# Fewer dummy matmuls, state weights over all rows, merged row sums and a new written-out order in a fused cross-attention and mixer kernel

## The chip, the core and the metric

The kernel runs on one core of a Trainium2 chip. The metric is the device time of one execution in microseconds, as the median of several runs; smaller is better. A profile of one execution gives a span (from the first to the last recorded instruction), and that execution has a time of its own, a little longer than its span.

The engines are named as in the profile: PE is TensorE's matrix multiply and PEld its loading of the stationary operand, DVE is VectorE, ACT is ScalarE, POOL is GpSimd, and SP is SyncE, which here only issues transfers.

## The reference

For each of 8 batches there are 8 heads with 512 tokens of x (64 wide) and 32 state rows (64 wide). Both directions of attention are computed, each as a plain softmax:

```python
scores = scale * np.matmul(x, state.transpose(0, 1, 3, 2))      # [8, 8, 512, 32]
a = softmax(scores); xread = np.matmul(a, state)
scores2 = scale * np.matmul(state, x.transpose(0, 1, 3, 2))     # the same products, transposed
a2 = softmax(scores2); sread = np.matmul(a2, x)
y = concat([xread, sread])  ->  [8, 544, 512]                    # heads side by side
wq = y @ w_q; wk = y @ w_k                                       # 512 -> 64
mixed = (scale * wq @ wk.T) @ y
out = np.maximum(mixed, 0.0) @ w_out                             # [8, 544, 512], float32
```

## The kernel before

Everything is done per batch b, in bfloat16 operands with float32 sums. The steps are small functions, and the kernel's whole order is a text, ORDER: a list of tokens `name.b.engine`. They are issued one by one, and each engine works through its own instructions strictly in that order, waiting where an operand or a buffer is not there yet. The last letter of a token says where or how: p is POOL, v DVE, a ACT, s a store by SP; for TensorE's steps t multiplies with a stationary operand of 128 columns, c with two of 64 columns side by side (the helpers `mm`, lines 161 and 163, and `tr`, lines 170 and 174), and r means that the step has one form only. There is no scheduler behind it: which work stands ahead of which on each engine is what the text says.

The steps of a batch are these. `ix` loads x through POOL's queue and casts it (for batch 0, four smaller loads and the casts `xc`). `xT0` and `xT1` transpose four heads each, eight 128x128 transposes, and `xTe` evicts them from PSUM. `pt0`, `pt1` are the scores, `exp0`, `exp1` their exponentials on ACT, without a maximum, into E. `rs` adds E over the 32 state rows on DVE (a token with a digit takes half of it, one without a digit all), `rinv` inverts the sums, and `A` on POOL multiplies: the attention of the tokens. `at` transposes A, `ate` evicts it. `sums` and `srd` make the attention of the state rows: column sums of E and E transposed times x. `srn` normalises them on DVE, `sbd` spreads them over blocks on POOL, `srT` transposes them.

The mixer doesn't form y for the tokens. It multiplies A with small matrices instead: `sw` (line 246) are the state rows times w_q and w_k, `wq`, `wk` and `wks` the projections, `g` is A transposed times wk, `v` combines it with the block-spread state (`stbd`, made once per batch on POOL) into a 64x512 matrix V, and `mix0`, `mix1`, `mixs` are V with wq, of which `mxe` and `mse` take the positive part. `fin0` to `fin3` multiply that with w_out, 128 tokens of 512 columns each, in four matmuls of 512 columns; two of them share a PSUM tile that `oe` evicts together and `os` stores with 512 KB. `fix` is the same for one piece, evicted and stored alone by `oc` with 256 KB; the very last piece (`oc3.7.b`) is halved between DVE and ACT. `fs` does the state rows of four batches at a time.

`stt` transposes the states of one to three batches; `ste` and `stf` evict its two halves into `stT`. In `stT` a head of the first half of the heads occupies rows 0 to 63, one of the second half rows 64 to 127, and the other 64 rows are zero (`zst`).

`fill` (line 155) issues dummy matmuls of zeros, 512 columns each, as many as the token's number. Their results aren't used.

PSUM is divided into two pools: psA with two tiles of two banks (dummies, `sw`, `mix` and `fin`), and psB with four of one bank (all else). A step that needs a tile waits until the former tenant of its place has been evicted. The single pieces pass through a pool in SBUF, tail, with seven buffers.

Of the kernel before, what the change touches and what calls it, by code (L numbers as in the profile page):

```python
# [13 lines left out]


ORDER = """
zst.0.p ix1.0.p stc.0.v xc1.0.a fill.1.t stt.0.c ste.0.v stbd.0.p stf.0.a xc0.0.p xc3.0.v ix2.0.p
fill.7.t xT0.0.t xc2.0.v xTe0.0.a fill.1.t xT1.0.t is.0.p stc.1.v fill.1.t stt.1.c xTe1.0.v stbd.2.p
fill.1.t pt0.0.t stf.1.v fill.1.t pt1.0.t exp0.0.a ste.1.v iwo.0.p exp1.0.a rs0.0.v fill.4.t
sums.0.t ix3.0.p rinv0.0.v wc.0.a fill.1.t xT0.1.t rs1.0.v fill.1.t srd.0.r xTe0.1.v A0.0.p fill.1.t  # L20
xT1.1.t fill.1.t sw.0.r xTe1.1.a rinv1.0.v fill.1.t pt0.1.t srn.0.v A1.0.p at0.0.t srT.0.t exp0.1.a
pt1.1.t srTe.0.v sbd.0.p swe.0.a xT0.2.t rs0.1.v at1.0.t exp1.1.a xT1.2.t xTe0.2.v stbd.1.p ate.0.a
xTe1.2.v fill.1.t stt.2.c stt.3.c rs1.1.v ste.2.a pt0.2.t stbd.6.p stf.3.v exp0.2.a fill.1.t wq.0.c
ste.3.v wks.0.c ix4.0.p stf.2.a wk.0.t rs0.2.v sw.3.r pt1.2.t wke.0.v swe.3.a stbd.3.p sw.1.r
rinv.1.v exp1.2.a g.0.t sw.2.r ge.0.v stbd.5.p swe.1.a rs1.2.v sums.2.t v.0.c wqe.0.a rinv.2.v
xT1.3.c swe.2.a A.1.p ve.0.v xT0.3.c xTe1.3.a srd.2.r xTe0.3.v mix0.0.r mix1.0.r mxe0.0.v sums.1.t
mxe1.0.a A.2.p srd.1.r at.1.t pt1.3.t srn.1.v ate.1.a fin0.0.t srn.2.v ix5.0.p xT1.4.t exp1.3.a
srT.1.t xT0.4.t xTe1.4.v srTe.1.a fin1.0.t sbd.1.p xTe0.4.a rs1.3.v pt1.4.t wq.1.c sbd.2.p exp1.4.a
wks.1.c wqe.1.v pt0.4.t oe0.0.a srT.2.t wk.1.t rs1.4.v at.2.t ix6.0.p fin2.0.t ate.2.v wke.1.a
os0.0.s exp0.4.a stbd.7.p g.1.t srTe.2.v fin3.0.t ge.1.v rs0.4.v sums.4.t stbd.4.p oe1.0.a srd.4.r  # L30
rinv.4.v v.1.c srn.4.v wq.2.c A.4.p ve.1.a os1.0.s srT.4.c wks.2.c wk.2.t srTe.4.a mixs.1.r wke.2.v
mix1.1.r wqe.2.a mix0.1.r mse.1.v xT1.5.t mxe0.1.a ix7.0.p at.4.t xTe1.5.v g.2.t xT0.5.t mxe1.1.a
ge.2.v sbd.4.p pt1.5.t xTe0.5.v v.2.c exp1.5.a fin2.1.c ve.2.v pt0.5.c rs1.5.v mixs.2.r mix1.2.r
exp0.5.a ate.4.v xT1.6.c mse.2.a sums.5.c fin3.1.c xTe1.6.a rs0.5.v rinv.5.v xT0.6.c mxe1.2.a
oe1.1.v A.5.p pt1.6.c wq.4.c srd.5.r exp1.6.a mix0.2.r srn.5.v os1.1.s fin0.1.c mxe0.2.a rs1.6.v
sbd.5.p xT0.7.c xTe0.6.v fin0.2.c xTe0.7.a wqe.4.v pt0.6.c srT.5.c at.5.c exp0.6.a xT1.7.c ate.5.v
srTe.5.a fin1.2.c xTe1.7.a rs0.6.v wq.5.c rinv.6.v wks.5.c wk.5.c wqe.5.a pt1.7.c A.6.p wke.5.v
wks.4.c sums.6.c exp1.7.a srd.6.r g.5.t oe0.2.a rs1.7.v wk.4.t pt0.3.t fin1.1.t srn.6.v exp0.3.a
os0.2.s wke.4.v sbd.6.p at.6.t oe0.1.a rs0.3.v srT.6.t g.4.t fin2.2.t ate.6.v os0.1.s fin3.2.t
ge.5.v ge.4.v srTe.6.v v.5.c oe1.2.a rinv.3.v wq.6.c ve.5.v A.3.p wks.6.c wk.6.c v.4.c os1.2.s  # L40
wke.6.a wqe.6.v mix1.5.r ve.4.a mixs.5.r mix0.5.r mxe1.5.v sums.3.t mxe0.5.a g.6.t srd.3.r mixs.4.r
ge.6.v mix0.4.r mse.5.a mix1.4.r srn.3.v mxe0.4.a v.6.c mse.4.v sbd.3.p srT.3.c pt0.7.c srTe.3.v
at.3.c mxe1.4.a ve.6.v fin2.5.c ate.3.v exp0.7.a fin3.5.c rs0.7.v wq.3.c oe1.5.a wks.3.c fin0.4.c
rinv.7.v A.7.p wqe.3.a os1.5.s mix0.6.r mixs.6.r wk.3.t mse.6.a fin1.4.t wke.3.a mxe0.6.a g.3.t
oe0.4.v at.7.t sums.7.t ate.7.a srd.7.r mix1.6.r srn.7.v os0.4.s fin2.4.c mxe1.6.v sbd.7.p srT.7.c
fin3.4.c srTe.7.a ge.3.v fin2.6.c oe1.4.v v.3.c fin3.6.c ve.3.v os1.4.s fin0.5.c oe1.6.a fin1.5.c
os1.6.s mix1.3.r oe0.5.v mixs.3.r wq.7.c mxe1.3.a wks.7.c wk.7.c mixs.0.r mse.3.v mix0.3.r os0.5.s
mse.0.a wke.7.v fin0.6.c wqe.7.a mxe0.3.a g.7.c fin1.6.c ge.7.a fin0.3.c oe0.6.v fin1.3.c os0.6.s
v.7.c oe0.3.a fin2.3.c ve.7.a fin3.3.c os0.3.s mix0.7.r oe1.3.a mixs.7.r fs.3.t mxe0.7.v mse.7.a
os1.3.s mix1.7.r fse.3.v fs.7.t mxe1.7.a fse.7.v fix1.7.t fix2.7.t oc1.7.a fix0.7.t oc2.7.a fix3.7.t  # L50
oc0.7.a oc3.7.b
"""


# [1 line left out]
def kernel(  # L56
# [20 lines left out]
    NP = H // 2  # L77
# [3 lines left out]

    const = ctx.enter_context(tc.tile_pool(name="const", bufs=1))
    work = ctx.enter_context(tc.tile_pool(name="work", bufs=4))
    tail = ctx.enter_context(tc.tile_pool(name="tail", bufs=7))
    psA = ctx.enter_context(tc.tile_pool(name="psA", bufs=2, space=bass.MemoryType.PSUM))
    psB = ctx.enter_context(tc.tile_pool(name="psB", bufs=4, space=bass.MemoryType.PSUM))

# [4 lines left out]
    stT = const.tile([128, B, 2, H, NS], BF, name="stT")  # L92
    stbd = const.tile([128, B, 2, NP, D], BF, name="stbd")
    w_f = const.tile([128, NP, 2, DH], FP, name="w_f")
    w_qk = const.tile([128, NP, 2, DH], BF, name="w_qk")
    w_o = const.tile([128, KC, DM], BF, name="w_o")
    sw = const.tile([128, B, 2, 2, DH], BF, name="sw")
# [143 lines left out]
    def sw_mm(n, p, e):  # L241
        ps = psA.tile([128, 2, 512], FP, name="sw_ps", tag="psA")
        for bb in range(2):
            for q in range(NP):
                for r in range(2):
                    nc.tensor.matmul(
                        out=ps[NS * q : NS * q + NS, r, 2 * DH * bb : 2 * DH * bb + 2 * DH],
                        lhsT=stT[64 * r : 64 * r + 64, 2 * p + bb, r, NP * r + q, :],
                        rhs=w_qk[64 * r : 64 * r + 64, q, 0:2, :],
                        start=True,  # L250
                        stop=True,
                    )
        G["sw", p] = ps
# [363 lines left out]
    def fs_ev(n, b, e):  # L617
# [7 lines left out]
        "zst": zeros, "stt": st_tr, "ste": st_ev, "stf": st_ev,  # L625
        "stbd": stbd_blk, "fill": fill, "fix": fin_mm, "os": fin_st,
        "sw": sw_mm, "swe": sw_ev, "xT": xT_mm, "xTe": xT_ev, "xs": x_dT, "as": a_dT, "pt": pt_mm, "exp": pt_exp,
        "rs": rs, "rinv": rv, "A": nrm, "at": at_mm, "ate": at_ev,
        "srd": srd, "sums": sums, "srn": srn, "sbd": sbd, "srT": srT_mm, "srTe": srT_ev,
# [38 lines left out]
```

## Time and profile before

| | us |
|---|---|
| median of 5 runs | 88.06 (87.75 to 88.66) |
| the profiled execution | 87.74 |
| its span | 86.0 |
| PE busy in the span | 80.2 (1579 matmuls) |
| DVE, ACT, POOL busy | 52.6, 56.0, 45.1 |
| dummy matmuls of `fill` | 23 |
| output written, from the first store's issue at 28.5 on | 8.91 MB |

The page shows busy times, a picture of the span in 40 slices, the chain of work that ended last, and groups of equal instructions with their mean length. A matmul's row shows the time from its start to its modelled end, and neighbours overlap; the distance from one group's start to the next is what the group costs in a stream. A shape such as 128*64 behind the tiles' names is that of the stationary operand: rows times columns.

### The profile page before, as it was taken

What the parts mean: (1) busy time and instruction counts of PE and PEld (TensorE: products, weight loads), DVE (VectorE), ACT (ScalarE), POOL (GpSimd) and SP (SyncE); (2) the same over time, 40 slices, a digit from 0 to 9 for tenths busy, and PEclk for the clock granted to TensorE, in tenths of its full rate; (3) what the DMA queues carried; (4) which work ended last, traced back from release to release, by engine and by line L of the source; (5) the groups of instructions that cost most, each with busy time, mean ns of one, the idle gap of its engine ahead of it and who ended that gap; (6) DMA issues with size and microseconds to landing.
All of it is one profiled execution on the core that took longest, in us unless ns stands there. A gap on an engine that the chain in (4) does not pass through costs nothing.

```text
span 86.0 us, 3560 instructions
## 1 busy us (share of the span) xinstructions
PE 80.2 (93%) x1579; PEld 53.1 (62%) x1579; DVE 52.6 (61%) x111; ACT 56.0 (65%) x83; POOL 45.1 (52%) x58
## 2 busy tenths in 40 slices
PE   4999999999999999999999999999999999999900
PEld 1336567778877688778689657865755565534400
DVE  2238864998956857887766958880687355055010
ACT  1634539989789678588887838968921591765530
POOL 7999979999999969308508653408050000000000
PEclk9999999999999999999999999999999999999999
DMA  0899999999519999992600565102362662567782
GB/s 10 284 324 188 199 193 192 198 189 162 82 12 150 132 138 345 273 165 31 252 0 11 213 278 208 44 8 111 133 236 95 274 280 105 238 250 293 294 312 78
DMA packets 15119, 15.00 MB, mean 175 GB/s; under 512 B 3712, under 2 KB 12672, under 8 KB 15104
## 3 DMA queue, kind: packets, MB, share of 16 engines
q0 software_dynamic: 9104, 4.36, 40.6%
q1 hardware_dynamic: 4880, 8.98, 28.2%
q10 hardware_dynamic: 1120, 1.44, 4.6%
q8 instruction: 12, 0.20, 0.9%
q14 instruction: 3, 0.02, 0.1%
HBM read 10.22 MB, written 8.91 MB: 223 GB/s over the span
## 4 chain that ended last, share of the span: by engine, by line
PE 79%; DMA 9%; ACT 4%; POOL 3%; issue 1%; DVE 1%; POOLq 0%
PE fin_ps L161 21%; PE fin_ps L163 12%; DMA x_bf<-in_x_dram 9%; PE mix_ps L541 5%; PE xT_ps L174 5%; PE xT_ps L170 3%; PE srd_ps L369 3%; PE at_ps L174 3%; PE v_ps L505 3%; PE fins_ps L163 2%; PE g_ps L163 2%; PE wq_ps L433 2%; PE v_ps L514 2%; POOL stT L201 2%; PE pt_ps L163 2%; PE wk_ps L163 2%
## 5 line engine op out<-in xcount | busy, mean ns | idle before, releaser
L346 POOL TENSOR_TENSOR A<-E,rinv 128x1024 bf16<-128x1024 bf16 (+1 forms) x9 | 15.4, 1720 | 11.8 <-DVE rinv L340 11.3
L161 PE MATMUL fin_ps<-w_o,rmix 128*64 128x512 bf16 x160 | 19.4, 380 | 0.0
L142 ACT COPY ost<-fin_ps 128x1024 f32<-128x1024 f32 (+2 forms) x13 | 11.2, 864 | 11.6 <-PE fin_ps L161 5.9
L148 ACT ACTIVATE rmix<-mix_ps 128x1024 bf16<-128x1024 f32 x12 | 12.1, 1024 | 2.5 <-PE mix_ps L541 2.4
L144 DVE COPY ost<-fin_ps 128x1024 f32<-128x1024 f32 (+1 forms) x6 | 6.5, 1091 | 9.9 <-PE fin_ps L163 5.4
L407 POOL TENSOR_TENSOR sbd<-srn,mask 128x256 bf16<-128x256 bf16 x16 | 9.4, 613 | 6.0 <-DVE srn L397 5.9
L161 PEld LDWEIGHTS <-rmix 128*64 128x64 bf16 x160 | 8.4, 110 | 6.2 <-issue 0.6
L163 PE MATMUL fin_ps<-w_o,rmix 128*128 128x512 bf16 x48 | 11.7, 379 | 0.0
L332 DVE TENSOR_REDUCE rsum<-E 128x16 f32<-128x512 bf16 x16 | 10.8, 675 | 0.9 <-ACT E L317 0.7
L317 ACT ACTIVATE E<-pt_ps 128x512 bf16<-128x512 f32 x16 | 9.5, 601 | 2.4 <-PE pt_ps L161 1.3
L234 POOL TENSOR_TENSOR stbd<-st_bf,mask 128x256 bf16<-128x256 bf16 x16 | 9.3, 610 | 0.4 <-DVE st_bf L144 0.2
L142 ACT COPY xT<-xT_ps 128x1024 bf16<-128x1024 bf16 x7 | 7.1, 1012 | 3.0 <-PE xT_ps L174 2.3
L144 DVE COPY xT<-xT_ps 128x1024 bf16<-128x1024 bf16 x9 | 6.2, 688 | 2.0 <-PE xT_ps L174 1.8
L155 PE MATMUL fill_ps<-zero 128*128 128x512 bf16 x23 | 7.3, 381 | 0.0
L150 DVE TENSOR_SCALAR rmix<-mix_ps 128x1024 bf16<-128x1024 f32 x4 | 4.9, 1222 | 3.4 <-PE mix_ps L541 3.4
L163 PEld LDWEIGHTS <-rmix 128*128 128x128 bf16 x48 | 4.3, 98 | 4.0 <-ACT rmix L148 0.2
L183 POOL DMA_DIRECT2D x_bf<-in_x_dram x7 | 6.6, 949 | 0.0
L174 PE MATMUL xT_ps<-ident,x_bf 128*128 128x128 bf16 x80 | 6.0, 219 | 0.3 <-ACT E L317 0.2
L174 PEld LDWEIGHTS <-x_bf 128*128 128x128 bf16 x80 | 4.9, 98 | 1.7 <-issue 0.5
L541 PE MATMUL mix_ps<-wq,V 64*128 64x256 bf16 x64 | 5.8, 272 | 0.0
L132 PE MATMUL warm_ps<-zero 128*128 128x512 bf16 x8 | 3.4, 597 | 1.2 <-DVE mask L133 1.2
L163 PE MATMUL pt_ps<-stT,xT 128*128 128x64 bf16 x88 | 4.4, 193 | 0.0
(90 smaller groups left out, 139.8 us busy)
## 6 DMA issues: line engine op xcount, KB each, us to landing
out_dram<-ost SPq DMA_DIRECT2D x14, 512.0 KB, 2.7
x_bf<-in_x_dram POOLq DMA_DIRECT2D x7, 512.0 KB, 7.7
out_dram<-ost ACTq DMA_DIRECT2D x3, 256.0 KB, 2.1
x_f<-in_x_dram ACTq DMA_DIRECT2D x2, 256.0 KB, 3.9
x_f<-in_x_dram SPq DMA_DIRECT2D x2, 256.0 KB, 4.3
w_o<-in_moe_w_out_dram POOLq DMA_DIRECT2D x1, 512.0 KB, 8.5
out_dram<-ost SPq DMA_DIRECT2D x2, 256.0 KB, 2.4
st_bf<-in_state_dram POOLq DMA_DIRECT2D x1, 160.0 KB, 7.9
```

The costliest lines, as they stand in the source:

```text
L142: nc.scalar.copy(out=out, in_=in_)
L144: nc.vector.tensor_copy(out=out, in_=in_)
L148: nc.scalar.activation(out=out, in_=in_, func=AF.Relu)
L161: nc.tensor.matmul(out=out[64 * h : 64 * h + 64], lhsT=lh, rhs=rhs, **kw)
L163: nc.tensor.matmul(out=out, lhsT=lhsT, rhs=rhs, **kw)
L174: nc.tensor.transpose(out=out, in_=in_, identity=ident)
L234: nc.gpsimd.tensor_tensor(out=stbd[:, b, r], in0=st_bf[:, b, r : r + 1, :].to_broadcast((128, NP, D)), in1=mask[:, :, None].to_broadcast(( ...
L317: nc.scalar.activation(out=L[b]["E"][:, r].rearrange("p c q n -> p c (q n)"), in_=L[b][f"pt{r}"], func=AF.Exp, scale=float(scale),)
L332: nc.vector.reduce_sum(out=L[b]["rsum"][:, w], in_=L[b]["E"].rearrange("p r c q n -> p (r c q) n")[:, w], axis=AX.X,)
L346: eng.tensor_tensor(out=L[b]["A"].rearrange("p r c q n -> p (r c q) n")[:, w], in0=L[b]["E"].rearrange("p r c q n -> p (r c q) n")[:, w], ...
L407: nc.gpsimd.tensor_tensor(out=L[b]["sbd"][:, r], in0=L[b]["srn"][:, r : r + 1, :].to_broadcast((128, NP, D)), in1=mask[:, :, None].to_broa ...
L541: nc.tensor.matmul(out=ps[:, h, kk, :], lhsT=L[b]["V"][rows, 128 * k : 128 * k + 128], rhs=L[b]["wq"][rows, 0:SH], start=True, stop=True,)
```

## The change

There are three edits.

1. The order text is a new one. It has 14 dummy matmuls instead of 23, none of them behind the first transposes of batch 1. For batches 3 to 7 the two half row sums `rs0`, `rs1` are one step `rs`. Of the output pieces, two each of batches 5 and 6 are now single ones (`fix`, `oc`) beside the four of batch 7, eight in all. Most steps change places, some the engine (a `v` for an `a` or the reverse), and some TensorE steps the form (t or c).
2. In `sw_mm` the stationary operand and the moving one span all 128 rows instead of the 64 that aren't zero.
3. The pool tail has 12 buffers instead of 7.

Nothing else differs; line numbers after the order text are lower by two.

The core of the diff, with the parts of the order that are spoken of:

```diff
-zst.0.p ix1.0.p stc.0.v xc1.0.a fill.1.t stt.0.c ste.0.v stbd.0.p stf.0.a xc0.0.p xc3.0.v ix2.0.p
-fill.7.t xT0.0.t xc2.0.v xTe0.0.a fill.1.t xT1.0.t is.0.p stc.1.v fill.1.t stt.1.c xTe1.0.v stbd.2.p
-fill.1.t pt0.0.t stf.1.v fill.1.t pt1.0.t exp0.0.a ste.1.v iwo.0.p exp1.0.a rs0.0.v fill.4.t
-sums.0.t ix3.0.p rinv0.0.v wc.0.a fill.1.t xT0.1.t rs1.0.v fill.1.t srd.0.r xTe0.1.v A0.0.p fill.1.t
-xT1.1.t fill.1.t sw.0.r xTe1.1.a rinv1.0.v fill.1.t pt0.1.t srn.0.v A1.0.p at0.0.t srT.0.t exp0.1.a
-pt1.1.t srTe.0.v sbd.0.p swe.0.a xT0.2.t rs0.1.v at1.0.t exp1.1.a xT1.2.t xTe0.2.v stbd.1.p ate.0.a
...
-v.7.c oe0.3.a fin2.3.c ve.7.a fin3.3.c os0.3.s mix0.7.r oe1.3.a mixs.7.r fs.3.t mxe0.7.v mse.7.a
-os1.3.s mix1.7.r fse.3.v fs.7.t mxe1.7.a fse.7.v fix1.7.t fix2.7.t oc1.7.a fix0.7.t oc2.7.a fix3.7.t
-oc0.7.a oc3.7.b
+zst.0.p ix1.0.p stc.0.v fill.1.t stt.0.c stbd.0.p stf.0.a ste.0.a xc1.0.a xc0.0.p xc3.0.v ix2.0.p
+fill.5.t xT0.0.t xc2.0.v fill.1.t xT1.0.t xTe0.0.v is.0.p stc.1.v fill.1.t pt0.0.t xTe1.0.v stbd.2.p
+fill.1.t stt.1.c exp0.0.a stf.1.v fill.1.t pt1.0.t ste.1.a rs0.0.v iwo.0.p exp1.0.a rinv0.0.v A0.0.p
+rs1.0.v fill.4.t xT0.1.t wc.0.a xT1.1.t rinv1.0.v sums.0.t xTe0.1.v A1.0.p srd.0.r sw.0.r xTe1.1.v
+at0.0.t swe.0.a pt0.1.t ix3.0.p srn.0.v at1.0.t xT0.2.t exp0.1.a ate.0.v srT.0.t sbd.0.p xT1.2.t
+xTe0.2.a srTe.0.v pt1.1.t xTe1.2.v wq.0.c exp1.1.a stbd.6.p wks.0.c rs0.1.v wk.0.t wqe.0.a stt.2.c
+wke.0.v sums.1.t ste.2.a stbd.1.p pt1.2.t stf.2.v g.0.t srd.1.r exp1.2.a ge.0.v sw.1.r srn.1.v
+ix4.0.p v.0.c swe.1.a rs1.1.v stt.3.c ve.0.a sw.2.r rinv.1.v sbd.1.p srT.1.t pt0.2.t stf.3.a swe.2.v
+mix0.0.r mixs.0.r exp0.2.a mix1.0.r mse.0.v A.1.p xT1.3.t ste.3.v mxe1.0.a sums.2.t srTe.1.v xT0.3.t
+xTe1.3.v srd.2.r mxe0.0.a sw.3.r xTe0.3.v ix5.0.p pt1.3.t at.1.t srn.2.v swe.3.a fin2.0.t rs1.2.v
...
+exp1.7.a ate.5.v exp0.7.a g.4.t at.6.t ge.4.v srT.6.t fin3.2.t srTe.6.v ate.6.v v.4.c oe1.2.v wq.6.c
+ve.4.a sums.7.c wq.5.c wks.5.c wqe.6.v wqe.5.a mix1.4.r os1.2.s mix0.4.r rs.7.v mxe1.4.a mixs.4.r
+srd.7.r wks.6.c wk.5.c wk.6.c wke.5.a fin2.3.c mxe0.4.v mse.4.a wke.6.a g.5.c fin3.3.c srn.7.v
+ge.5.a rinv.7.v sbd.7.p srT.7.c v.5.c oe1.3.v srTe.7.a g.6.c ve.5.a fin0.3.c A.7.p ge.6.v fin1.3.c
...
+wke.7.v mix0.6.r wqe.7.a mix1.6.r mxe0.6.v fix3.5.c mxe1.6.a fix2.5.c mse.5.v fse.3.v g.7.c fin0.6.c
+ge.7.a oc2.5.v fin1.6.c oc3.5.v fin0.5.c oe0.6.a fin1.5.c os0.6.s v.7.c oe0.5.a fix2.6.c ve.7.v
+os0.5.s mixs.6.r mixs.7.r oc2.6.a mix1.7.r mse.6.v mix0.7.r mse.7.v mxe1.7.a fix3.6.t mxe0.7.v
+fs.7.t oc3.6.a fix2.7.t fse.7.a fix1.7.t oc2.7.a fix0.7.t oc1.7.a fix3.7.t oc0.7.a oc3.7.b
...
-    tail = ctx.enter_context(tc.tile_pool(name="tail", bufs=7))
+    tail = ctx.enter_context(tc.tile_pool(name="tail", bufs=12))
...
-                        lhsT=stT[64 * r : 64 * r + 64, 2 * p + bb, r, NP * r + q, :],
-                        rhs=w_qk[64 * r : 64 * r + 64, q, 0:2, :],
+                        lhsT=stT[:, 2 * p + bb, r, NP * r + q, :],
+                        rhs=w_qk[:, q, 0:2, :],
```

## The prediction

> **What bounds the kernel now.** I read the page's busy times first, then the chain that ended last, then TensorE's instructions in order of time.
>
> ```profile
> PE 80.2 (93%) x1579; PEld 53.1 (62%) x1579; DVE 52.6 (61%) x111; ACT 56.0 (65%) x83; POOL 45.1 (52%) x58
> PE   4999999999999999999999999999999999999900
> PEclk9999999999999999999999999999999999999999
> ```
>
> TensorE is busy in every slice but the first and the last two, at full clock; no other engine passes 65%. The chain in order of time says where it is held and where it runs free:
>
> ```profile
> 3.00 7.73 DMA x_bf<-in_x_dram
> ...
> 10.77 0.62 PE xT_ps L174 x8
> ...
> 78.42 3.47 PE fin_ps L163 x16
> 81.89 0.02 issue
> 81.92 0.44 DVE ost L144
> ...
> 82.38 0.37 ACT ost L142
> ```
>
> The reader should see three parts: 10.77 us until the second batch of x has landed (issued by POOL at 3.00), 71.1 us of TensorE, and 4.1 us from 81.89 to the span's end at 86.0 for the last eviction and its store. The windows confirm the middle (width, then busy time and count of TensorE, its weight loads, DVE, ACT and POOL):
>
> ```profile
> 10.77:20.50 9.73, 9.41 (x246) 7.13 (x248) 7.42 (x17) 8.02 (x14) 9.14 (x15) 1.00 1.48 188
> 30.00:40.00 10.00, 10.00 (x282) 8.14 (x282) 7.83 (x15) 7.92 (x12) 5.64 (x6) 1.00 1.09 205
> 70.00:81.90 11.90, 11.88 (x106) 5.66 (x102) 3.74 (x4) 6.92 (x11) 0.00 (x0) 1.00 0.62 245
> ```
>
> So the end moves with TensorE's own work, plus waits, after 10.77. TensorE's timeline prices that work, by the distance from one group's start to the next:
>
> ```profile
> 18.33 0.31 PE L246 MATMUL sw_ps<-w_qk,stT 64*32 64x128 bf16 x16
> 18.57 0.41 PE L163 MATMUL pt_ps<-stT,xT 128*128 128x64 bf16 x8
> 18.90 0.31 PE L246 MATMUL sw_ps<-w_qk,stT 64*32 64x128 bf16 x16
> ...
> 31.40 0.39 PE L433 MATMUL wq_ps<-AT,sw 128*64 128x256 bf16 x4
> 31.62 0.28 PE L442 MATMUL wq_ps<-srT,w_qk 128*64 128x32 bf16 x8
> ...
> 46.74 0.40 PE L163 MATMUL wk_ps<-sw,AT 128*128 128x64 bf16 x8
> 46.98 0.40 PE L163 MATMUL pt_ps<-stT,xT 128*128 128x64 bf16 x8
> 47.21 1.03 PE L163 MATMUL fin_ps<-w_o,rmix 128*128 128x512 bf16 x4
> 48.08 0.61 PE L174 MATMUL at_ps<-ident,A 128*128 128x128 bf16 x8
> ```
>
> pt takes 0.23 us (46.98 to 47.21) where its neighbours use the array whole (128*128), but 0.33 (18.57 to 18.90) before a group in the shape 64*32. Each change of this shape (written after the tiles' names) costs about 0.105 us. With that one number and a base per group (fin 0.865, xT and at 0.447, pt, wk and g 0.23 whole or 0.25 in halves, mix 0.225, v 0.44, wq 0.335, wks 0.13, srd 0.25, sw 0.135, dummy 0.216) I added up the order from 10.77: 64.30 of groups and 54 changes x 0.105 = 5.67 give 80.74. The trace ends at 81.89; the 1.15 between are 0.17 for the last matmul's run-out, some 0.6 of waits before 20.5 (0.34 for an exponential at 14.42, 0.3 at 17.7) and 0.36 of small ones later. The sum follows the trace within 0.1 from 20.5 to 70, so I trust it for the new order.
>
> **What the Trainium skill says.** "TensorEngine Tiling (Array Packing)", section Tiling Modes (Key Properties): changing the tiling mode, not just the tile, drains TensorE. The trace agrees, at 0.105 us, also between column modes. "TensorE: Matmul & The Clock Gate", section Part 2 (Back-to-back issue gap): N/2.4 + 2.5 ns warm, 56 ns for N=128; eight xT transposes in 0.45 us agree. Its Part 1 says that an idle window of about 3.4 us halves the clock; the clock row shows none. "Runtime: NRT & Kernel Launch", section Instruction fetch mechanics: instructions come in 16 KiB blocks of 256, ahead of use. The page's 12 instruction packets of 0.20 MB agree; their 0.9% of 16 engines' span is 1.03 us each, and TensorE spends over 3 us on a block. No wait of before needs fetch as its cause, so I give the "instruction fetch" side of the new order nothing, in either direction (at most 0.3 if one late block was inside the small waits).
>
> **The change part by part.**
>
> *Dummies.* 23 become 14. Three of the nine lie before 10.77, where the x load holds TensorE: nothing. The six later ones are 6 x 0.216 = 1.30 of stream. sums.0 (0.18) moves from before 10.77 to after it. Ahead of it ACT now evicts the first state before it casts its share of x (done about 6.4, not 4.8), but the first exponential still starts near 8.5 and A for batch 0 near 10.5; the cover is the x load's 10.77, with 0.3 to spare.
>
> *Order after 10.77.* Shape changes fall from 54 to 41: 13 x 0.105 = 1.37. Of these, three lie ahead of xT1.3 (the first transposes of batch 3) and ten behind it. Halved and whole groups trade for a few hundredths.
>
> *Column-tiled state weights (L246).* sw now contracts all 128 rows (the other half of stT is zero), in shape 128*32. Before, r=0 and r=1 ran in different row tiles: 16 matmuls in 0.135. Now r, the innermost loop, puts two successive matmuls on the same 32 columns, and matmuls start in order: per bb and q one 53 ns stream more, 8 x 53 = 0.43 us. The trace does not show this form; bounds are 0.21 (four abreast throughout, 16 x 53 / 4) and 0.85 (one by one). I take 0.43: +0.30 each, three times ahead of xT1.3, once behind. That it stands next to srd (also 128*32) saves shape changes, counted above.
>
> *Merged row sums.* Five pairs of L332 (675 ns each for 512 elements) become one of 1024. DVE's ost evictions take 0.686 for 512 and 1.224 for 1024 elements, so 0.54 for the second half: 1.21 instead of 1.35. DVE has room: nothing by itself, but a longer piece ahead of what is queued behind it, see below.
>
> *Moved loads.* ix3 is now behind both halves of A for batch 0 on POOL, issued about 12.7 instead of 9.89. It took 10.3 us to land (20.2), behind the w_o load (issued 9.08, landed 17.6) on one queue; from 12.7 it is still queued before w_o has landed, so again 20.2. The cover is w_o; without it, the 6.6 to 7.7 us of the other x loads still give 20.4 at worst. ix6 and ix7 come at 28.8 and 34 by POOL's list (A 1.91, sbd 1.19, stbd 1.18, load 0.94 each), landing about 36 and 41.4; TensorE wants them at 37.1 and 42.0. Little slack.
>
> *Late pieces singly, deeper tail buffers.* Two more pairs of pieces (batches 5 and 6) go through psB singly: two 512 KB stores become four of 256, two evicted by DVE and stored by SP, two by ACT (0.59, and 0.36 of issue on its queue). SP's list holds stores alone, in the order of their evictions, so none stands long behind a later one. At the end ACT is through with its last whole piece when DVE is through with its half of the split one, as before: the 4.1 us tail stays. I take nothing, bounded by -0.2 (less in flight) and +0.3 (the last 14 pieces now come in 13.4 us, 274 GB/s, near the 312 that the page reaches).
>
> *Sum to xT1.3.* New order from 10.77: 7.13 of groups, 12 changes (1.26), 0.89 for three slower sw: 20.05. Waits: 0.2 for batch 2 (5.86 + 7.7 = 13.56), and at the end the buffer of pt0.2, freed by its exponential, which on ACT stands behind a state eviction, sw and V: ACT finishes at 20.45. So xT1.3 starts at 20.5, where it started before (20.50). The 1.3 us of dummies are spent on slower sw and on waits that the dummies had covered.
>
> *Sum behind it.* Before 60.86. New 56.02 + 29 x 0.105 + 0.30 = 59.36: 1.50 less. New waits, laid out by each queue's list: at g.5, whose PSUM slot was held by srd of batch 7 until srn.7. DVE needs from fin3.2's end: 0.2, ost 1.22, wq 0.45, merged row sum 1.21, rmix 1.22, srn 0.45, some 0.1 of queue: 4.85; TensorE has 4.19 of other work: 0.7 wait. At fin2.1, for rmix of batch 2 on ACT: 0.15. Small waits as before, 0.36. Behind g.5 on TensorE stand fin3.3 and all that follows.
>
> TensorE's end: 20.5 + 59.36 + 0.7 + 0.15 + 0.36 + 0.17 = 81.24, against 81.89: **0.65 less**. The profiled execution took 87.74 (span 86.0 and 1.7 around it), so 87.1; the median of the runs is 88.06, 0.32 above it, so **87.4** on that scale.
>
> **The rivals.**
>
> *All of the gain arrives.* sw runs four abreast (0.21), so xT1.3 waits only for batch 3, at 20.25; DVE's chain at g.5 fits. 20.25 + 59.14 + 0.36 + 0.17 = 79.92, 1.97 less: 86.1. For it: DVE has 52.6 us of work in 86, and TensorE hardly waited anywhere in the old order. Against: the in-order start of pairs on one tile, and the 4.85 against 4.19.
>
> *The x loads become the bound: slower.* On POOL ix6 and ix7 stand behind A and sbd, which wait for DVE (A waited 11.3 us in all for rinv). Place: the first transposes of batch 7. Up to a landing at 42.0 nothing is lost; each 0.1 later is 0.1 on the end. If ix7, issued at 34, takes 10.3 us as ix3 did, with outputs written beside it, it lands at 44.3: 2.3 of wait, less 0.65 gained: 89.7. It ends on the slower side at a landing past 42.65, by over 1% past 43.5. Against: the later loads took 6.6 to 7.7.
>
> *The change doesn't do what it says:* fewer dummies leave gaps and the clock drops. No gap in my lists is over 0.8 us, so I leave it no chance of its own.
>
> **How the numbers follow.** Forecast 0.48 (own range 86.8 to 88.0), full gain 0.35, late loads 0.17. One per cent, about what a measurement of this kernel can tell, is 87.18 or 88.94. Faster: 0.35 and 0.3 of the forecast's 0.48, 0.49. Slower: 0.14 of the late loads' 0.17. Within: 0.37. The range runs from 85.8 (full gain and a little less waiting than before) to 88.8, leaving out about 0.1 on each side.
>
> **What would show it.** Right: changes of shape still 0.1 each; sw x16 of 0.43 from start to start; xT1.3 near 20.5; TensorE idle for DVE's srn ahead of g.5 near 56; TensorE's end near 81.2. Wrong: sw at 0.2; idle time on x_bf near 42; slices of the clock row below 9; instruction packets followed by idle TensorE.

## The result, and the profile after

The changed kernel takes 88.38 us (median of 44 runs, 87.57 to 91.39) against 88.11 us for the kernel before (79 runs, 87.58 to 90.11). The ratio is 1.0008, with a 95% interval of 0.9991 to 1.0025: no difference that can be measured, where 0.7 us less was forecast. The profiled execution of the changed kernel took 87.89 us with a span of 86.1; the one before, 87.74 and 86.0. Some executions of each kernel fall into a slower state; the medians count all executions and the ratios leave the slow ones out, and as the profiled execution of three kernels below (w_out later, 64 places further on, srn.7 ahead) is a slow one, their rows are read for their place more than for their length.

Busy times and slices of the page, after:

```profile
PE 78.9 (92%) x1532; PEld 52.9 (61%) x1532; DVE 54.9 (64%) x107; ACT 52.6 (61%) x84; POOL 45.0 (52%) x58
PE   4999999799999999979999999999999999999900
PEclk9999999999999999999999999999999999999998
```

TensorE has 1.3 us less to do (78.9 instead of 80.2), at full clock, so the work that was to go did go. But two slices that held a 9 now hold a 7. The windows (width, then busy time and count of TensorE, its weight loads, DVE, ACT and POOL) show how much is idle there:

```profile
10.77:20.50 9.73, 9.02 (x273) 7.74 (x273) 8.26 (x20) 7.04 (x12) 8.73 (x13) 1.00 1.38 173
30.00:40.00 10.00, 9.51 (x225) 7.62 (x221) 7.53 (x12) 8.37 (x15) 7.40 (x9) 1.00 1.05 159
70.00:81.60 11.60, 11.60 (x108) 5.76 (x104) 4.40 (x8) 6.55 (x10) 0.00 (x0) 1.00 0.63 242
```

0.71 us in the first window (0.32 before) and 0.49 in the second (none before). The chain that ended last, in order of time, has them as rows of its own:

```profile
16.51 0.18 PE srd_ps L161 x4
16.69 0.64 issue
17.33 0.25 PE srd_ps L161 x4
...
21.11 0.04 issue
21.15 0.61 PE xT_ps L172 x8
...
37.14 0.31 PE pt_ps L161 x7
37.45 0.49 issue
37.94 0.20 PE pt_ps L161
...
57.41 0.30 DVE srn L395
57.71 0.04 issue
57.76 0.44 PE g_ps L159 x16
...
78.17 3.47 PE fin_ps L161 x16
81.64 0.02 issue
81.67 0.43 DVE ost L142
82.10 0.02 issue
82.12 0.37 ACT ost L140
```

"issue" means that TensorE waited for nothing that the profile shows. Both stretches fall inside a group: the column sums of batch 1 stop after four of eight equal matmuls, the last `pt1.4` before its eighth matmul, with all operands there. TensorE ends at 81.64 (81.24 forecast, 81.89 before), and from there to the span's end it is 4.46 us (4.1 before). So two things stand against the gain: 1.13 us idle inside TensorE's stream and about 0.4 behind it.

The place of the two stretches gives the clue. Counted through TensorE's program, each matmul with its weight load as two and with three instructions of other kinds at the start, they stand at instructions 450 and 1474. These differ by 1024, four blocks of 256, and each instruction packet that the profile counts has 16 KB. The Trainium skill, "Runtime: NRT & Kernel Launch", section Instruction fetch mechanics, says that such a block holds 256 instructions and that the next one is fetched while the current one runs. The DMA view of the changed kernel, ahead of the second idle time (queue, packets, MB, and the sum of the packets' times as a share of 16 engines' time, which passes 100% where packets overlap):

```profile
q0 software_dynamic: 797, 0.41, 93.9%
q1 hardware_dynamic: 90, 0.37, 27.4%
```

This is from 32.2, when TensorE enters the block ahead (instruction 1218), to 35.7. On q0 is batch 6's x, on q1 an output store of 512 KB that SP issued at 30.13 (from 30 to 34 q1 moved 0.02 MB); not one instruction packet moves. The same view from 35.7 to 36.7:

```profile
q0 software_dynamic: 107, 0.05, 42.4%
q1 hardware_dynamic: 51, 0.15, 40.4%
q8 instruction: 1, 0.02, 5.9%
```

The load and the store are ending, and the packet (q8) goes, at 35.71. TensorE runs on at 37.94, 2.23 later. For instruction 450 it is the same: block ahead entered at 11.99, packet at 15.05, running on at 17.33 (2.28 later). In the trace of before the corresponding packets went at 14.69 and 34.79, so their blocks were due at about 16.95 and 37.05, and TensorE wanted them at 17.32 and 37.64: late by neither, with 0.4 and 0.6 us to spare. The new order has shorter work in each block and later loads.

**Theory:** a block of instructions that TensorE needs is held back by a load of x or w_out on its way. **Rivals:** the stretches are waits for data that the trace doesn't name; or the loss is in the form of `sw` or the removed dummies.

### The profile page after: what moved, and what is told of

It is laid out like the page before. It is cut to its first block, busy times and chain, and to the rows that moved or that the text cites. A ratio compares the mean times of both kernels' runs of the same rounds, so it can differ in the third digit from the quotient of the medians.

```text
span 86.1 us, 3462 instructions
## 1 busy us (share of the span) xinstructions
PE 78.9 (92%) x1532; PEld 52.9 (61%) x1532; DVE 54.9 (64%) x107; ACT 52.6 (61%) x84; POOL 45.0 (52%) x58
## 4 chain that ended last, share of the span: by engine, by line
PE 69%; DMA 7%; DVE 6%; SPq 4%; ACT 3%; issue 3%; POOL 2%; ACTq 0%; DVEq 0%
PE fin_ps L159 18%; PE fin_ps L161 12%; DMA w_f<-in_moe_w_k_dram 7%; PE xT_ps L172 4%; PE mix_ps L539 4%; PE pt_ps L161 3%; PE at_ps L172 3%; POOL A L344 2%; PE srd_ps L367 2%; SPq L121 2%; PE wk_ps L161 2%; PE xT_ps L168 2%; PE fins_ps L161 2%; PE wq_ps L431 2%; DVE ost L142 2%
## 5 line engine op out<-in xcount | busy, mean ns | idle before, releaser
L159 PE MATMUL fin_ps<-w_o,rmix 128*64 128x512 bf16 x152 | 18.1, 380 | 0.0
L142 DVE COPY ost<-fin_ps 128x1024 f32<-128x1024 f32 (+2 forms) x8 | 7.8, 990 | 7.0 <-PE fin_ps L161 4.7
L330 DVE TENSOR_REDUCE rsum<-E 128x16 f32<-128x512 bf16 (+1 forms) x11 | 10.0, 920 | 1.9 <-ACT E L315 1.7
L146 ACT ACTIVATE rmix<-mix_ps 128x1024 bf16<-128x1024 f32 x9 | 9.2, 1032 | 1.6 <-PE mix_ps L539 1.5
L148 DVE TENSOR_SCALAR rmix<-mix_ps 128x1024 bf16<-128x1024 f32 x7 | 8.5, 1220 | 1.1 <-PE mix_ps L539 1.1
L172 PE MATMUL xT_ps<-ident,x_bf 128*128 128x128 bf16 x96 | 7.0, 219 | 0.1
L140 ACT COPY xT<-xT_ps 128x1024 bf16<-128x1024 bf16 x6 | 6.1, 1017 | 1.4 <-PE xT_ps L172 1.1
L161 PE MATMUL pt_ps<-stT,xT 128*128 128x64 bf16 x112 | 5.6, 193 | 0.5 <-issue 0.5
L142 DVE COPY AT<-at_ps 128x1024 bf16<-128x1024 bf16 x6 | 4.1, 688 | 2.6 <-PE at_ps L168 2.4
L161 PEld LDWEIGHTS <-xT 128*128 128x128 bf16 x112 | 4.4, 98 | 1.6 <-issue 0.8
```

Of the source, the lines that this page charges most:

```text
L140: nc.scalar.copy(out=out, in_=in_)
L142: nc.vector.tensor_copy(out=out, in_=in_)
L146: nc.scalar.activation(out=out, in_=in_, func=AF.Relu)
L159: nc.tensor.matmul(out=out[64 * h : 64 * h + 64], lhsT=lh, rhs=rhs, **kw)
L161: nc.tensor.matmul(out=out, lhsT=lhsT, rhs=rhs, **kw)
L172: nc.tensor.transpose(out=out, in_=in_, identity=ident)
```

## Experiments

### Without the later loads of x, in both kernels

```diff
-    x_bf = [const.tile([128, H, NC * D], BF, name=f"x_bf{b}") for b in range(B)]
+    x_bf = [const.tile([128, H, NC * D], BF, name=f"x_bf{b}") for b in range(2)]
+    x_bf += [x_bf[1]] * (B - 2)
...
+            if b >= 2:
+                return
```

> The changed kernel without the six POOL loads of x for batches 2 to 7; those batches compute on batch 1's x, so part of the input is left out and the output is another. Theory (instruction fetch): TensorE's two idle stretches of 0.64 us (near 16.7, in the row sums of batch 1) and 0.49 us (near 37.5, in pt1 of batch 4) are the arrival of the next block of instructions, held up by the x loads on the same DMA engines. Without the loads both fall below 0.15 us, TensorE's end comes some 1.0 us earlier than 81.64, and the time is 86.7 to 87.1, a ratio to the kernel before of 0.985 to 0.990. Rival (data): the stretches are waits for operands or PSUM places that the profile didn't catch; they stay within 0.2 us of their size and the ratio is 0.996 to 1.002.

> The kernel before without the same six loads, on batch 1's x likewise (part of the input left out). Theory (instruction fetch): the kernel before reaches each block later than it arrives, so nothing is gained: ratio 0.995 to 1.002, against 0.985 to 0.990 for the changed kernel without loads; the difference of the two, about 1 us, is what the new order is worth when instructions are there. Rival (data): removing the loads helps both orders alike, their ratios differ by less than 0.004.

The changed kernel: 86.64 us, ratio to the kernel before 0.9796 (0.9733 to 0.9860, from three executions). The kernel before: 87.88, ratio 0.9971 (0.9948 to 0.9994). So without these loads the change is worth 1.75%; the two profiled executions, 86.66 and 87.64, differ by 1.1%. In the changed kernel's chain only one of the two stretches is left:

```profile
16.08 0.98 issue
```

The block of instruction 1474 now went at 32.21, 0.28 after TensorE entered the block ahead of it at 31.93, and nothing stood idle near 37. The DMA view from 32 to 33 has little else:

```profile
q8 instruction: 1, 0.02, 7.2%
q1 hardware_dynamic: 12, 0.00, 0.6%
```

The output store had passed too: it moved from 30.7 to 32.0. So this run takes away the load and the store that it held up, and doesn't tell them apart. The first stretch stayed and grew, against what I expected of it. Its packet went at 14.74, when w_out, the last load on its way in this kernel, ended. It wasn't the later x that had held it. Some 0.35 of the gain is another thing, 4.1 instead of 4.46 us from TensorE's end to the span's end: with fewer loads, the list of waits that closes the program is shorter (below).

### Batch 6's x issued 1.1 us sooner

```diff
-fin1.0.t wke.1.a sbd.3.p srTe.3.a at.2.t rinv.3.v oe0.0.a xT1.4.t ix6.0.p ate.2.v g.1.t xT0.4.t
+fin1.0.t wke.1.a ix6.0.p sbd.3.p srTe.3.a at.2.t rinv.3.v oe0.0.a xT1.4.t ate.2.v g.1.t xT0.4.t
```

> Edit: on GpSimd's queue the load of batch 6's x is issued ahead of batch 3's block-diagonal sums instead of behind them, 1.1 us sooner; all else stays. Theory (fetch waits for loads): this load ends about 1.1 us sooner, so the block of instruction 1474, asked for at 32.2, leaves at about 34.5 instead of 35.71, is usable at 36.8 and is wanted at 37.45: the 0.49 us idle before the last pt1.4 falls below 0.1 and TensorE ends 0.4 to 0.5 us sooner; the first stretch (0.64 us in sums.1) stays. Ratio to the kernel before 0.994 to 0.997. Rival (a wait for data): 0.49 us stays, ratio 1.000 to 1.002.

87.28 us, ratio 0.9873 (0.9807 to 0.9939, from three executions). On POOL the issue of a load and a step of work (`sbd.3`) change places, and TensorE's timeline has no gap before the last `pt1.4` any more:

```profile
36.80 0.50 PE L161 MATMUL pt_ps<-stT,xT 128*128 128x64 bf16 x8
37.14 0.34 PE L161 MATMUL srd_ps<-ones,E 128*128 128x1 bf16 x8
```

The packet went at 34.88, and TensorE ended at 80.80, 0.84 sooner than in the trace of after. Of this, 0.27 was there ahead of the moved load: this execution ran on from the first stretch at 17.06 instead of 17.33. So the trace gives the edit 0.57 us. The first stretch stands at 0.60, as expected. The measured gain, 1.3%, is larger than that and than the 0.3 to 0.6% I expected (the interval ends just short of 0.994). The second stretch isn't the same in every execution, 0.73 and 0.77 in two kernels below with the same loads, but that doesn't cover all of it; the rest stays open.

### w_out issued behind batch 3's x

```diff
-fill.1.t stt.1.c exp0.0.a stf.1.v fill.1.t pt1.0.t ste.1.a rs0.0.v iwo.0.p exp1.0.a rinv0.0.v A0.0.p
+fill.1.t stt.1.c exp0.0.a stf.1.v fill.1.t pt1.0.t ste.1.a rs0.0.v exp1.0.a rinv0.0.v A0.0.p
...
-at0.0.t swe.0.a pt0.1.t ix3.0.p srn.0.v at1.0.t xT0.2.t exp0.1.a ate.0.v srT.0.t sbd.0.p xT1.2.t
+at0.0.t swe.0.a pt0.1.t ix3.0.p iwo.0.p srn.0.v at1.0.t xT0.2.t exp0.1.a ate.0.v srT.0.t sbd.0.p xT1.2.t
```

> Edit: on GpSimd's queue the load of w_out is issued behind batch 3's x instead of ahead of A of batch 0; TensorE, VectorE, ScalarE keep their program. Theory (fetch waits for loads): when the block of instruction 450 is asked for at 12.0, only x of batch 2 and the states are on their way, so it leaves at about 14 instead of 15.05 and is usable at 16.3, ahead of 16.6: the 0.64 us at 16.69 falls below 0.1. Batch 3's x is issued 0.8 us sooner and lands at about 20.2 instead of 20.9, so xT1.3 starts at 20.3 to 20.5 instead of 21.15; TensorE's end 80.9 to 81.1, ratio to the kernel before 0.991 to 0.996. w_out is then issued at about 13.4 and lands by 22, ahead of its first use at 23.6. Rival 1 (the stretch is a wait for data): 0.64 us stays, ratio 1.000. Rival 2 (the x of batch 3 takes the place of w_out in the way of the fetch): packet near 15 as now, 0.6 us stays, ratio 0.999 to 1.001.

90.58 us, ratio 1.0102 (1.0063 to 1.0140): slower. The stretch at instruction 450 went as expected: packet at 13.84, TensorE there at 16.30 without a pause. But another opened one block on, at instruction 706, as its timeline shows:

```profile
20.53 0.61 PE L172 MATMUL xT_ps<-ident,x_bf 128*128 128x128 bf16 x8
20.97 0.17 PE L161 MATMUL srd_ps<-ones,E 128*128 128x1 bf16 x1
22.73 0.33 PE L161 MATMUL srd_ps<-ones,E 128*128 128x1 bf16 x7 [1.59 <-issue]
```

The block ahead of that one was entered at 16.30, with batch 3's x and w_out issued at 13.11 and 14.04, and the packet went at 20.36. The DMA view of this kernel from 16.4 to 20.3 has q0 alone:

```profile
q0 software_dynamic: 1077, 0.71, 129.8%
```

So fetch behind loads fits here too, and my edit only moved the harm to the next block, against all I expected of the time. The stretch at instruction 1474 stayed, at 0.55. The first row above is of use too: with no stretch ahead of it, `xT1.3` started at 20.53, where the prediction had put it.

### Every TensorE instruction 64 places further on

```diff
-fill.5.t xT0.0.t xc2.0.v fill.1.t xT1.0.t xTe0.0.v is.0.p stc.1.v fill.1.t pt0.0.t xTe1.0.v stbd.2.p
+fill.37.h xT0.0.t xc2.0.v fill.1.t xT1.0.t xTe0.0.v is.0.p stc.1.v fill.1.t pt0.0.t xTe1.0.v stbd.2.p
...
-            nc.tensor.matmul(out=ps, lhsT=zero[:, 0:128], rhs=zero, start=True, stop=True)
+            w = 64 if e == "h" else 512
+            nc.tensor.matmul(out=ps[:, 0:w], lhsT=zero[:, 0:128], rhs=zero[:, 0:w], start=True, stop=True)
```

> Edit: the five dummy matmuls of 512 columns ahead of batch 0's first transposes become 37 of 64 columns, so that every later instruction of TensorE stands 64 places further on in its program; the work, its order and all waits stay. Theory (instructions are fetched in blocks of 256, and a block that is asked for while a load of x or w_out is on its way comes only when that load has ended): the idle stretches stay at TensorE's instructions 450 and 1474, which are now 64 places earlier in the work. The first block is asked for at about 9.9 us, waits for the loads on their way until about 14, is usable 2.25 us later, 16.3, and is wanted at 15.3: about 1 us idle in wq.0/wks.0 instead of 0.64 in sums.1. The second is asked for at about 31.2, waits for batch 6's load until about 35.3, is usable at 37.5 and is wanted at 35.5: about 2 us idle in wks.3 instead of 0.49 before the last pt1.4. Ratio to the kernel before 1.012 to 1.025. Rival (the stretches are waits for data that the trace does not show): they stay in sums.1 and pt1.4 with their 0.64 and 0.49 us; ratio 1.000 to 1.003.

91.61 us, ratio 1.0241 (1.0148 to 1.0333), inside my range and far from the rival's. Its timeline has two rows behind a pause:

```profile
21.45 0.28 PE L245 MATMUL sw_ps<-w_qk,stT 128*32 128x128 bf16 x2 [2.18 <-issue]
...
41.19 0.28 PE L458 MATMUL wk_ps<-w_qk,srT 128*64 128x64 bf16 x5 [2.00 <-issue]
```

The stretches left the column sums and `pt1.4`, which now run through, and stand in other steps: at instructions 706 and 1474. A wait for data would have stayed with its data. One half was not as I wrote: at 450 the packet left at 12.89 already and the pause was 0.1; the one that came late was the next, held from 15.26 to 19.00 by w_out and batch 3's x.

The packets of all these kernels side by side (us; "entered" is when TensorE starts the block ahead; "wanted" is when it would go on without a pause):

```
kernel               instruction  entered  packet  wanted  goes on
before                       450    11.58   14.69   17.32    17.32
after                        450    11.99   15.05   16.69    17.33
no later x, after            450    11.77   14.74   16.08    17.06
before                      1474    31.80   34.79   37.64    37.64
after                       1474    32.20   35.71   37.45    37.94
no later x, after           1474    31.93   32.21   36.98    36.99
x6 sooner                   1474    31.93   34.88   37.0     37.10
w_out later                  706    16.30   20.36   21.14    22.73
64 further on                706    15.26   19.00   19.27    21.45
64 further on               1474    34.36   38.87   39.20    41.19
```

Where TensorE had to wait, it went on 2.2 to 2.5 us after the packet's start.

What holds a packet isn't loads alone. In the kernel after, the packet for instruction 1986 went at 44.29, 1.67 after TensorE entered the block ahead at 42.62, and in between one output store moved and nothing else:

```profile
q1 hardware_dynamic: 139, 0.51, 77.7%
```

In the kernel before nothing moved at this place, and the packet went after 0.24 (42.45 to 42.69). This block was early enough in both. But at instruction 1474 batch 6's load and the store behind it both lie ahead of the packet, in the kernel with x6 sooner too, and no run here separates their shares.

### State weights in the old form

```diff
-                        lhsT=stT[:, 2 * p + bb, r, NP * r + q, :],
-                        rhs=w_qk[:, q, 0:2, :],
+                        lhsT=stT[64 * r : 64 * r + 64, 2 * p + bb, r, NP * r + q, :],
+                        rhs=w_qk[64 * r : 64 * r + 64, q, 0:2, :],
```

> Edit: the kernel after with the state weights' products in the old form (slices of 64 rows of weights instead of 128). By my prediction's price (0.43 us for a new group) the old form, at 0.24 to 0.31, would be 0.1 to 0.2 us a group quicker and the kernel about 0.3 us faster, ratio 0.997. By the duration in the changed kernel's trace (0.25 us a group, and where a group follows the row sums' 32-row pieces no change of tile shape between them) the old form is 0.0 to 0.1 us a group slower: ratio 1.000 to 1.004.

88.25 us, ratio 0.9986 (0.9945 to 1.0027): no difference that can be told, and the interval holds both expectations. The traces decide: the chain gives a group 0.23 us in the old form and 0.25 to 0.28 in the new one.

### The kernel before without its six later dummies

```diff
-sums.0.t ix3.0.p rinv0.0.v wc.0.a fill.1.t xT0.1.t rs1.0.v fill.1.t srd.0.r xTe0.1.v A0.0.p fill.1.t
-xT1.1.t fill.1.t sw.0.r xTe1.1.a rinv1.0.v fill.1.t pt0.1.t srn.0.v A1.0.p at0.0.t srT.0.t exp0.1.a
+sums.0.t ix3.0.p rinv0.0.v wc.0.a fill.1.t xT0.1.t rs1.0.v srd.0.r xTe0.1.v A0.0.p 
+xT1.1.t sw.0.r xTe1.1.a rinv1.0.v pt0.1.t srn.0.v A1.0.p at0.0.t srT.0.t exp0.1.a
...
-xTe1.2.v fill.1.t stt.2.c stt.3.c rs1.1.v ste.2.a pt0.2.t stbd.6.p stf.3.v exp0.2.a fill.1.t wq.0.c
+xTe1.2.v stt.2.c stt.3.c rs1.1.v ste.2.a pt0.2.t stbd.6.p stf.3.v exp0.2.a wq.0.c
```

> The kernel before with its six dummies behind xT0.1 left out, 1.30 us of TensorE, nothing else changed. Theory (instruction fetch): the block of instructions that starts at instruction 450 arrives near 16.9 and TensorE, without five of the six dummies, gets there near 16.3: an idle stretch without a releaser of 0.4 to 0.8 us appears at that instruction, and with the known waits for exponentials the time falls by at most 0.5 us: ratio 0.994 to 1.000. Rival (dummies are plain cost): no such stretch, TensorE's end comes 1.0 to 1.3 us earlier, ratio 0.985 to 0.989. Second rival (dummies covered waits for data): no gain either, but the idle stretches have a releaser (an exponential, a load, POOL's A).

88.04 us, ratio 0.9945 (0.9915 to 0.9976). In its timeline the work behind `xT0.1` runs up to 0.9 us sooner than before, and gives all of it back at the first transposes of batch 3, which start at 20.52 (20.50 with the dummies). From there on each matmul lies 0.07 later than in the trace of before, to the end:

```profile
19.39 0.39 PE L514 MATMUL v_ps<-stbd,G 128*64 128x256 bf16 x4
20.52 1.08 PE L170 MATMUL xT_ps<-ident,x_bf 128*64 128x128 bf16 x32 [0.75 <-DMA x_bf<-in_x_dram]
```

The dummies lay beside a load: this is the second rival's picture. The pause without a releaser that I expected at instruction 450 didn't come; TensorE stood 0.34 near it, at 16.51, for an exponential. Where the half per cent of the measured ratio comes from, this trace doesn't show; that stays open.

### The last store, and the list that closes the program

At its end SP waits, in a fixed order, for eight semaphores that the transfers of SP and ACT signal in turn, and for others paired with them; a wait that is already satisfied takes 0.06 us. There are 33 such transfers after and 31 before. Before, the last one signals the seventh of the eight, so one more wait follows when it lands. After, it signals the first, and seven follow. From the issue of the last store to the span's end it was 3.2 us before and 3.6 after; in the execution without the later x, which closes with six waits, 3.2. The last store itself isn't later: it had landed 3.1 us after TensorE's end in both (85.01 before, 84.75 after, as SP's waits show). Seven more loads turn the last store to the last place:

```diff
+    spare = const.tile([128, 7, D], FP, name="spare")
...
+        if (n, b) == ("os0", 0):
+            for i in range(7):
+                nc.sync.dma_start(out=spare[:, i : i + 1], in_=st_src[:, i : i + 1])
```

> The changed kernel with seven more loads of 32 KB of the state into an unused tile, issued on SP behind the first output store. Theory (closing list of waits): the eight semaphores of the SP and ACT transfers are used in turn, and SP waits for all eight in a fixed order at the end, 0.06 us each; in the changed kernel the last store has the first one of the list, so seven waits follow its landing, in the kernel before one pair. With seven more transfers the last store has the last semaphore: the stretch from TensorE's end to the span's end shrinks from 4.46 to about 4.05 us, ratio to the kernel before about 0.997 (0.993 to 0.999). Rival (store backlog: more and smaller stores at the end land late): the stretch stays at 4.4 or more, ratio 1.000 to 1.004.

87.72 us, ratio 0.9938 (0.9912 to 0.9963), 0.7% under the changed kernel with seven transfers more. TensorE ended at 81.89, the span at 85.8: 3.9 instead of 4.46. Both idle stretches were there (0.63 and 0.73). From the last store's issue it was 3.0.

### srn.7 ahead of the copy of a mix

```diff
-srd.7.r wks.6.c wk.5.c wk.6.c wke.5.a fin2.3.c mxe0.4.v mse.4.a wke.6.a g.5.c fin3.3.c srn.7.v
+srd.7.r wks.6.c wk.5.c wk.6.c wke.5.a fin2.3.c srn.7.v mxe0.4.v mse.4.a wke.6.a g.5.c fin3.3.c
```

> Edit: on VectorE the division of batch 7's ratio sums (srn.7) is done ahead of the copy of half a mix of batch 4 (mxe0.4) instead of behind it; nothing else moves. Theory (g.5 waits for the bank that srn.7 frees, at the end of VectorE's queue): srd.7 is ready at 55.9, srn.7 is done by 56.6 instead of 57.7, g.5 starts when fin2.3 ends, at 57.4 instead of 57.76; TensorE's end and the span 0.35 us shorter, ratio to the kernel before 0.995 to 0.998. Rival (the copy of the mix, now 0.4 us later, holds a bank that is wanted as soon): another wait of 0.2 to 0.4 us stands at fin3.3 or behind, ratio 0.999 to 1.002.

87.97 us, ratio 0.9967 (0.9943 to 0.9992), as expected. Both idle stretches are there, at 0.52 and, in this execution, 1.30. In its timeline `g.5` follows `fin2.3` at the ordinary 0.86:

```profile
57.84 1.03 PE L159 MATMUL fin_ps<-w_o,rmix 128*64 128x512 bf16 x8
58.70 0.42 PE L159 MATMUL g_ps<-wk,A 128*64 128x64 bf16 x16
58.95 0.82 PE L159 MATMUL fin_ps<-w_o,rmix 128*64 128x512 bf16 x6
```

### The three together

```diff
-fin1.0.t wke.1.a sbd.3.p srTe.3.a at.2.t rinv.3.v oe0.0.a xT1.4.t ix6.0.p ate.2.v g.1.t xT0.4.t
+fin1.0.t wke.1.a ix6.0.p sbd.3.p srTe.3.a at.2.t rinv.3.v oe0.0.a xT1.4.t ate.2.v g.1.t xT0.4.t
...
-srd.7.r wks.6.c wk.5.c wk.6.c wke.5.a fin2.3.c mxe0.4.v mse.4.a wke.6.a g.5.c fin3.3.c srn.7.v
+srd.7.r wks.6.c wk.5.c wk.6.c wke.5.a fin2.3.c srn.7.v mxe0.4.v mse.4.a wke.6.a g.5.c fin3.3.c
...
+    spare = const.tile([128, 7, D], FP, name="spare")
...
+        if (n, b) == ("os0", 0):
+            for i in range(7):
+                nc.sync.dma_start(out=spare[0:1, i : i + 1], in_=st_src[0:1, i : i + 1])
```

> Edit: the kernel after with batch 6's x issued sooner, srn.7 ahead of mxe0.4, and seven loads of 256 bytes (spare, of no use) on SP's queue behind the first stored pair, so that the last store signals the last semaphore of the list that is waited for at the end. Theory: the three savings add: 0.49 (fetch at instruction 1474), 0.37 (g.5), 0.3 to 0.4 (closing list), 1.15 to 1.25 us together: TensorE's end near 80.3 to 80.6, from there to the span's end 4.0 instead of 4.46, ratio to the kernel before 0.985 to 0.989. Rival (what is saved ahead of it is taken by another block of instructions that then comes late, as when w_out was moved): an idle stretch of 0.3 us or more appears at the next boundary of 256 instructions, ratio 0.990 to 0.995.

86.78 us, ratio 0.9826 (0.9788 to 0.9864), faster than both kernels. From TensorE's end (81.02) to the span's end it is 3.98. Two stretches remain:

```profile
17.32 0.25 PE L162 MATMUL srd_ps<-ones,E 128*128 128x1 bf16 x4 [0.63 <-issue]
37.62 0.20 PE L162 MATMUL pt_ps<-stT,xT 128*128 128x64 bf16 x1 [0.18 <-issue]
```

No new one appeared at the blocks behind. TensorE's end itself is later than the 80.3 to 80.6 I expected, mainly because 0.18 of the second stretch is left and this execution was later from its start than the one with x6 sooner (17.32 instead of 17.06 behind the first stretch).

## Why the prediction was wrong

The step that failed is the one on instruction fetch: "nothing, in either direction (at most 0.3 if one late block was inside the small waits)". TensorE stood idle for 1.13 us in its place; some 0.7 of that was to be had at its end, 0.49 and, as shown below, 0.2. I had reasoned from a packet's own 1 us and from a block lasting over 3 us, and from no wait of before needing that cause. What I didn't look at is when the packets went. In the trace of before, too, the packets of 450 and 1474 left 3 us after their block's predecessor was entered, behind loads and, at 1474, stores, with 0.4 and 0.6 us to spare. That was a resource close to its limit without a wait. My list of signs did have the packets followed by idle TensorE, and that is the sign that came. The Trainium skill, "DMA: Bandwidth & Descriptors", section Queues, rings and completion order, says that a DMA engine goes round between the queues that have work, one packet of typically 9 to 17 descriptors at a time. If a packet of q0 in the profile, 0.06 to 0.1 us long, is one descriptor, which no run here shows, a turn would be an estimated 0.5 to 1.7 us by that page. Here packets left 2.1 to 4.5 us after the block ahead was entered where loads ran, and the measurement decides. It isn't the whole load that has to end either. At 15.05 about half of w_out had moved (some 260 of its 512 packets), and the microsecond from there on is still full of it:

```profile
q0 software_dynamic: 187, 0.19, 115.9%
```

What exactly lets a packet through stays open.

Term by term, for TensorE's end (81.24 forecast, 81.64 measured):

- *Up to `xT1.3`: 20.5, measured 21.15.* The mechanism named, the buffer freed by `pt0.2`'s exponential at 20.45 behind sw and V on ACT, is right. The chain after has exactly these ACT steps just ahead of 21.15, and without the stretch of 0.64 the start was 20.53. The stretch at 450 passed whole into it: +0.65. If that stretch alone went, batch 3's x would hold TensorE next. TensorE's weight loads waited for it until 20.94, so 0.2 us is what could be had, and the forecast start would have been missed by some 0.4 without any late block: ix3 was issued at 13.34, not 12.7, because A came later.
- *Column-tiled `sw`, 0.43: mis-sized.* It takes 0.25 to 0.28. In the timeline below, the next group starts 0.36 behind it, of which some 0.105 is the change of shape. That is near the 0.21 of four abreast, not the 0.43 of pairs one by one. Ahead of `xT1.3` ACT's chain sets the time and nothing is gained; behind it, one group, about -0.18.

```profile
18.00 0.42 PE L367 MATMUL srd_ps<-x_bf,E 128*32 128x64 bf16 x32
18.25 0.43 PE L244 MATMUL sw_ps<-w_qk,stT 128*32 128x128 bf16 x16
18.61 0.41 PE L503 MATMUL v_ps<-sbd,wk 128*64 128x512 bf16 x2
```

- *Changes of shape and groups behind `xT1.3`: right.* 60.74 was forecast with all waits, 60.49 measured. With the stretch at 1474 (+0.49), the smaller waits at `g.5` (-0.33) and `fin2.1` (-0.15) and the one `sw` (-0.18), -0.08 is left over.
- *`g.5` behind the merged row sum and `srn.7`: right in place, too long.* DVE's list came as laid out, at 1.12 for the merged sum, 1.13 for rmix and 1.20 for ost (each from the end of the step before it), and `g.5` waited 0.37 instead of 0.7.
- *The dummies: right.* They had covered waits. In the kernel before it is a load that they lay beside. The cover at the start was thinner than I said: the first exponential began at 9.03 and A at 11.26, not 8.5 and 10.5, and TensorE took the second half of A only when it was done, at 13.45.
- *Moved loads: in time for the data, batch 3's only because TensorE was late itself.* It landed at 20.9, not 20.2; batches 6 and 7 caused no wait. The rival of late loads was right that the new places of ix3 to ix7 on POOL's queue are where the gain can be lost, but the data was not what came late.

*The tail, "stays", bounded by -0.2 and +0.3:* 4.46 instead of 4.1, outside the bounds. Which semaphore the last store signals had no place in my list. Together: +0.40 at TensorE's end and +0.36 behind it on the 87.1 forecast for the profiled execution make 87.86; it took 87.89.

Without the two late blocks and the closing list the rival in which all of the gain arrives would have been near: 86.1 there, 86.78 measured with three small repairs and the first stretch still standing.

## What to carry to other kernels

In an unrolled program of thousands of instructions, list the times of the instruction packets and compare each with the moment when its block is wanted; where large loads or stores run, the margin can be half a microsecond, and denser work uses it up. An idle row with no releaser in the middle of equal instructions points there: count instructions and see whether the places differ by multiples of 256. The cure that worked here was on the load's queue, not in the idle engine's order, and the block after had to be looked at too. In this kernel, adding or removing a transfer on SP or ACT shifts which semaphore the last store signals, and with it some tenths at the end.

## What the runs showed that I had not expected

A block of instructions can be used 2.2 to 2.5 us after its packet's start, though the packet itself takes about 1 us. With no transfer on its way it left at most 1.2 us after TensorE entered the block ahead, 0.28 at instruction 1474 without the later x; with one 512 KB store and no load, 1.67; with the loads of the table, 2.1 to 4.5. Moving one load ahead of one step on POOL measured 1.3% faster (three executions, 0.57 us of it in the trace), and 64 more instructions, which lie ahead of 10.77 us where TensorE waits for x anyway, measured 2.3% slower than the changed kernel (two executions).
